# Loading the first two weight pieces behind the second attention group, and converting them behind groups 4 and 5

## The chip, the core and the metric

The kernel runs on one core of a Trainium2 chip. The metric is the device time of one execution in microseconds (us). Engines are named as in the profile: PE (matmuls), PEld (its weight loads), DVE (VectorE), ACT (ScalarE), POOL (GpSimd), SP (SyncE, which issues nearly all DMAs here). An engine's queue of issues is SPq, PEq and so on.

## The reference

An attention over (batch 4, heads 8, sequence 576, head dimension 64), half of the heads with a window of 32 keys, half with 32 keys at a distance of 4, is followed by two feed-forward layers of 512 -> 2048 -> 512 on its 2304 tokens:

```python
scores = scale * q @ k^T, masked; attn = softmax(scores); x = attn @ v
h = x @ w_in;  x = (maximum(h, 0) + alpha * minimum(h, 0)) @ w_out
h = x @ w2_in; x = (piecewise square of h) @ w2_out
```

## The kernel before

**Attention** is cut into 24 groups of three blocks. The first six groups (batch 0, `NGB` = 6, `GS` = 3) run at the start, each through the same steps: `e_scores` (PE), `e_exp` (maximum and subtract on DVE, L190 and L191, exponential on ACT, L193), `a_turn` (transposes on PE, copy on ACT, L214), `e_values` (48 small matmuls and as many weight loads on PE, L205, then `a_norm` on DVE, L229 to L231, which writes the tile `o`), `a_out` (transposes on PE, L238, copy on ACT into the big tile `XA`, L256). The score tile `s2` and the value tile `o2` have one PSUM buffer each, so the scores of a group wait until the subtract of the group before has read its tile. The loop at L804 interleaves the groups: turn i holds the scores and the exponential of group i, the transposes and the values of group i-1, the output of group i-2.

**The order is written by hand** (`manual_schedule`): every engine runs its instructions in the order of the code, and a wait at the head of an engine's queue holds up all that is behind it.

**Weights** come as 512 KB pieces of 64-bit integers. `w_load` issues a piece's DMA into a staging tile `st`, taking one of five buffers from `st_free`. `w_make` gives the three DVE steps that turn it into float32 (L321, L322, L315); `conv(k)` runs k such steps, and where a piece is finished its buffer goes back and `more()` may load the next. The last step of an input-weight piece puts it on a list; `w_cut()` then runs `w_split` for it: a copy on ACT (L327, the high half) and a subtract on POOL (L328, the low half) into a tile `wr`. `x_split` does the same for tiles of `XA`, giving `xv`. `f_h(n, f, (c,))` multiplies chunk c of weight piece f by an X tile: three PE matmuls (L513 to L515) on 128x512.

**Around the change.** Before the loop, SP is given the inputs of the six groups (`a_load_qk`, `a_load_v`, some 806 KB per group, tiles `e_in`), and behind groups 0 and 2 (`FIRST`, L58, L756) the first two weight pieces. In the loop, turns 0 and 2 end in `conv(3)` (L816), which converts one piece each. Turn 3 also splits the first X tile, clears a tile on POOL (L821) and gives SP the inputs of group 6 and all further weight pieces for which there are buffers. Turn 4 splits the second X tile. After the loop `f_h(n0, 0, (0,))` and `f_h(n0, 1, (0,))` need the two pieces; group 5's transposes, values and outputs are interleaved with the next chunks, and the main loop of slots begins, in which DVE converts the other pieces.

Of the kernel before, what the change touches and what calls it, by code (L numbers as in the profile page):

```python
# [10 lines left out]
F32 = mybir.dt.float32  # L11
# [43 lines left out]
NX = 9  # L55
NR = 4

FIRST = (0, 2)  # L58

EARLY = (5, 6)  # L60
READY = 12
# [26 lines left out]
def attention_then_two_ffns(ctx: ExitStack, tc: tile.TileContext, a0, aqk, av, w1i, w1o, w2i, w2o, alpha, masks, ident, out, out_l):  # L88
    nc = tc.nc
# [24 lines left out]
    sc_t, s_t, pT_t, o_t = {}, {}, {}, {}  # L114
# [3 lines left out]
    def a_load_qk(i):  # L118
        if i < NGB:
            nc.sync.dma_start(e_in[i][:, :QK], a0[i, :, :QK])  # L120
        elif i < NG:
            t = qk[i % 2]
            nc.sync.dma_start(t[:D, :QK], aqk[i - NGB, :D])
            nc.sync.dma_start(t[D:, KW:], aqk[i - NGB, D:])

    def a_load_v(i):
        if i < NGB:
            nc.sync.dma_start(e_in[i][:, QK:], a0[i, :, QK:])
        elif i < NG:
            for h in range(2):  # L130
                r = slice(h * D, (h + 1) * D)
                nc.sync.dma_start(vz[i % 2][r, :, h].rearrange("p n j d -> p n (j d)"), av[i - NGB, r])
# [34 lines left out]
    def e_scores(i):  # L167

        ps = ps_e.tile([P, 2, TW], F32, tag="s2", name="s_ps")
        t = e_in[i]  # L170
        mk = mask[:, i * GS:(i + 1) * GS]
        for h in range(2):
            nc.tensor.matmul(ps[:, h, :GS * KEYS].rearrange("p (n k) -> p n k", n=GS), idb, mk, start=True, stop=False)
        for n in range(GS):
            for j in range(4):
                r = slice(j * SUB, (j + 1) * SUB)
                k0 = _key_offset(i, 4 * n + j)
                for h in range(2):
                    p = slice(h * D, (h + 1) * D)
                    q = t[p, KW + n * P + j * SUB:KW + n * P + (j + 1) * SUB]  # L180
                    nc.tensor.matmul(ps[r, h, n * KEYS:(n + 1) * KEYS], q, t[p, k0:k0 + KEYS], start=False, stop=n == GS - 1)
        sc_t[i] = ps

    def e_exp(i):
        ps = sc_t.pop(i)
        s = buf(i, "s").rearrange("p (n k) -> p n k", k=KEYS)
        src = ps[:, :, :GS * KEYS].rearrange("p h (n k) -> p h n k", n=GS)
        mx = st_p.tile([P, 2 * GS], F32, tag="mx", name="mx")
        mx = mx.rearrange("p (h n) -> p h n", h=2)
        nc.vector.tensor_reduce(mx, src, AX.X, ALU.max)  # L190
        nc.vector.tensor_tensor(  # L191
            s.rearrange("p (n h) k -> p h n k", h=2), src, mx[:, :, :, None].to_broadcast([P, 2, GS, KEYS]), ALU.subtract)
        nc.scalar.activation(s, s, AF.Exp, scale=SCALE)  # L193
        s_t[i] = s

    def e_values(i):
        pT = pT_t.pop(i)
        ps = ps_e.tile([P, 2, TW], F32, tag="o2", name="o_ps")
        v = e_in[i][:, QK:].rearrange("p (n j d) -> p n j d", n=GS, j=4)
        for n in range(GS):  # L200
            for j in range(4):
                r = slice(j * SUB, (j + 1) * SUB)
                for h in range(2):
                    p = slice(h * D, (h + 1) * D)
                    nc.tensor.matmul(ps[r, h, n * DS:(n + 1) * DS], pT[p, n, r], v[p, n, j], start=True, stop=True)  # L205
        a_norm(i, ps[:, :, :GS * DS].rearrange("p h (n d) -> p n h d", n=GS))

    def a_turn(i, pool, tag):
        s = s_t.pop(i)
        ps = pool.tile([P, GS, P], F32, tag=tag, name="t_ps")  # L210
        for n in range(GS):
            nc.tensor.transpose(ps[:, n], s[:, 2 * n:2 * n + 2].rearrange("p h k -> p (h k)"), idt)  # L212
        pT = buf(i, "pT").rearrange("p (n k) -> p n k", k=P)
        nc.scalar.activation(pT, ps, AF.Copy)  # L214
        pT_t[i] = pT
# [10 lines left out]
    def a_norm(i, ps):  # L226
        o = tmp(i).tile([P, GS, 2, D], F32, tag="o", name="o")
        rs = st_p.tile([P, GS, 2, 1], F32, tag="rs", name="rs")
        nc.vector.tensor_scalar(rs, ps[:, :, :, D:], 1e-9, None, ALU.add)  # L229
        nc.vector.reciprocal(rs, rs)  # L230
        nc.vector.tensor_tensor(o, ps[:, :, :, :D], rs.to_broadcast([P, GS, 2, D]), ALU.mult)  # L231
        o_t[i] = o

    def a_out(i, pool, tag):
        o = o_t.pop(i)
        ps = pool.tile([P, GS * P], F32, tag=tag, name="x_ps")
        for n in range(GS):
            nc.tensor.transpose(ps[:, n * P:(n + 1) * P], o[:, n].rearrange("p h d -> p (h d)"), idt)  # L238
        b = i // NGB
        sb0 = (i % NGB) * GS  # L240
        subs = [x for n in range(GS) for x in _subs(sb0 + n)]
        at = 0
        while at < len(subs):
            hp, s0 = subs[at]
            n = 1
            while at + n < len(subs) and subs[at + n][0] == hp:
                n += 1
            src = ps[:, at * SUB:(at + n) * SUB]
            xb = X[hp][:, b * S:(b + 1) * S]
            p0, p1 = s0 * SUB, (s0 + n) * SUB  # L250
            if hp < NHP // 2:
                dst = xb.rearrange("p (r i) -> p i r", r=DIL)[:, p0 // DIL:p1 // DIL]
                src = src.rearrange("p (i r) -> p i r", r=DIL)
            else:
                dst = xb[:, p0:p1]
            nc.scalar.activation(dst, src, AF.Copy)  # L256
            at += n
# [7 lines left out]

    st_free = [f"v{i}" for i in range(NX - NST, NX)]

    def w_load(ph, f, part):
        w = ((w1i, w1o), (w2i, w2o))[ph][part]
        tag = st_free.pop(0)  # L270
        st = xv_p.tile([P, DM, 2], I32, tag=tag, name="st") if tag in xv_tags else pools[tag].tile([P, DM, 2], I32, tag=tag, name="st")
        nc.sync.dma_start(st.rearrange("p a b -> p (a b)"), w[f].bitcast(I32))
        cv[ph, f, part] = (st, tag)

# [83 lines left out]
    def w_split(n, f):  # L358
        t = r_slot((n, f))
        two(t[:, 0], t[:, 1], wi[n[0], f], nc.vector if n == PAIRS[0] and f < 2 else nc.gpsimd)  # L360
        wt[n, f] = t
        b = base.get((n[0], f // 2))
        if b:
            b[1] -= 1
            if not b[1]:
                x_free.append(b[0])

    def w_cut():
        while cut:
            w_split(*cut.pop(0))  # L370
# [51 lines left out]
    def x_split(n, c, on_pool=False):  # L422
        ph, t = n
        t0, w = TILES[ph][t]
        at = 0
        if w < TW and c % 2:
            x, at = xt[n, c - 1][0], w
        else:
            x = x_slot(n)
        two(x[:, 0, at:at + w], x[:, 1, at:at + w], X[c][:, t0:t0 + w], nc.gpsimd if on_pool else nc.vector)  # L430
        xt[n, c] = (x, at)
# [291 lines left out]
    def pieces(ph):  # L723

        return [(ph, 0, 0), (ph, 1, 0)] + [x for f in range(NF) for x in ((ph, f + 2, 0), (ph, f, 1)) if x[1] < NF]
# [4 lines left out]
    with tc.manual_schedule(), ExitStack() as late:  # L730
# [19 lines left out]
        pend_l = pieces(0)  # L750
        pend_w = list(pend_l)

        for i in range(NGB):
            a_load_qk(i)
            a_load_v(i)
            if i in FIRST:  # L756
                w_load(*pend_l.pop(0))
            if i == 1:
                nc.sync.dma_start(mask[:, 2 * GS:], masks[:, 2 * GS:])
        nc.sync.dma_start(al, alpha)  # L760
# [11 lines left out]
        def fill(n):  # L772

            for _ in range(n):
                nc.tensor.matmul(warm_ps, warm[:, :P], warm, start=True, stop=True)
# [11 lines left out]
        def conv(k):  # L787

            for _ in range(k):
                if not todo and pend_w and pend_w[0] in cv:  # L790
                    todo.extend(w_make(*pend_w.pop(0)))
                if todo:
                    todo.pop(0)()
                    if not todo:
                        more()
# [8 lines left out]
        for i in range(NGB):  # L804
            e_scores(i)
            if i >= 1:
                a_turn(i - 1, ps_a, "a")
            e_exp(i)
            if i >= 2:
                a_out(i - 2, ps_a, "w")  # L810
            else:
                fill(2)
            if i >= 1:
                e_values(i - 1)
            w_cut()
            if i in FIRST:  # L816
                conv(3)
            if i == 3:
                x_split(n0, 0, True)

                nc.gpsimd.memset(qk[0], 0.0)  # L821
                hold = False
                a_load_qk(NGB)
                w_load(*pend_l.pop(0))
                w_load(*pend_l.pop(0))
                a_load_v(NGB)
                more()
            if i == 4:
                x_split(n0, 1, True)
# [394 lines left out]
```

## Time and profile before

| | us |
|---|---|
| median of 3 runs | 848.47 (847.82 to 849.39) |
| profiled execution, its own time | 848.41 |
| span of its instructions | 846.3 |
| PE busy | 831.4 (98%) |
| DVE busy | 514.4 (61%) |
| ACT busy | 459.3 (54%) |
| POOL busy | 483.1 (57%) |
| mean granted TensorE clock | 0.996 |

The span runs from the first to the last instruction; 2.1 us of the execution's own time lie outside. A share of busy time is a mean over stages with different limits: the start, with small attention tiles and the first weights, is the only part in which PE is not busy throughout. Times of rows are us from the start of the span. A chain piece called "issue" is time in which the engine waited for nothing that the profile shows. The releaser in brackets is inferred. Matmul ends are modelled.

### The profile page before, as it was taken

The numbers are of one execution on the slowest core, as the hardware profiler recorded it, in microseconds if no ns is written. First come the engines' busy times: TensorE is split into PE (matmuls) and PEld (weight loads), VectorE is DVE, ScalarE is ACT, GpSimd is POOL, SyncE is SP. The second block draws the span as 40 slices with busy tenths as digits, with TensorE's granted clock in tenths as the row PEclk, the third lists the DMA queues.
The fourth block names the chain that finished last, engine by engine and source line by source line (L and its number), as shares of the span: only waits on it lengthen the run. The fifth ranks groups of instructions, "written<-read, shape, count | busy, mean of one in ns | idle before, by whom it ended". The sixth has DMA issues, their size and how long they took to land.

```text
span 846.3 us, 14045 instructions
## 1 busy us (share of the span) xinstructions
PE 831.4 (98%) x5232; PEld 681.3 (81%) x5234; DVE 514.4 (61%) x831; ACT 459.3 (54%) x883; POOL 483.1 (57%) x411
## 2 busy tenths in 40 slices
PE   6999999999999999999999999999999999999998
PEld 3667778998777878888888888888888888888897
DVE  4798787666775676776688565665326556530132
ACT  3444444665435465555444677675437666553375
POOL 2465656777434677767448676754662332346485
PEclk9899999999999999999999999999999999999999
DMA  8788665864640025444287735343835553538120
GB/s 303 240 252 228 203 171 179 257 196 135 191 129 26 1 75 180 144 154 169 100 312 301 282 142 204 127 173 121 327 125 203 196 198 125 174 134 313 69 82 25
DMA packets 54978, 147.43 MB, mean 174 GB/s; under 512 B 5632, under 2 KB 13440, under 8 KB 54912
## 3 DMA queue, kind: packets, MB, share of 16 engines
q1 hardware_dynamic: 54624, 146.39, 50.9%
q8 instruction: 41, 0.67, 0.3%
q14 instruction: 25, 0.20, 0.1%
q10 hardware_dynamic: 288, 0.16, 0.1%
HBM read 101.97 MB, written 44.56 MB: 173 GB/s over the span
## 4 chain that ended last, share of the span: by engine, by line
PE 92%; DVE 4%; ACT 1%; issue 1%; DMA 1%; ACTq 0%; DVEq 0%
PE y L706 14%; PE y L707 14%; PE y L708 14%; PE h_ps L544 9%; PE h_ps L546 9%; PE h_ps L545 9%; PE h_ps L513 5%; PE h_ps L515 5%; PE h_ps L514 5%; PE o_ps L223 2%; PE s_ps L149 1%; PE t_ps L212 1%; PE y L691 1%; PE y L692 1%; PE y L693 1%
## 5 line engine op out<-in xcount | busy, mean ns | idle before, releaser
L328 POOL TENSOR_TENSOR wol<-wo,woh 128x512 fp32r<-128x512 f32 x153 | 201.8, 1326 | 74.5 <-ACT woh L327 64.4
L328 POOL TENSOR_TENSOR wr<-wb,wr 128x512 fp32r<-128x512 f32 x60 | 77.8, 1297 | 130.3 <-ACT wr L327 130.3
L706 PE MATMUL y<-gh,wol 128*128 128x512 f32 (+1 forms) x384 | 146.3, 381 | 0.0
L708 PE MATMUL y<-gl,woh 128*128 128x512 f32 (+1 forms) x384 | 142.8, 372 | 0.0
L707 PE MATMUL y<-gh,woh 128*128 128x512 f32 (+1 forms) x384 | 142.8, 372 | 0.0
L328 POOL TENSOR_TENSOR wr<-wi,wr 128x512 fp32r<-128x512 f32 x50 | 64.6, 1293 | 121.2 <-ACT wr L327 119.9
L544 PE MATMUL h_ps<-xv,wr 128*128 128x512 f32 x336 | 131.3, 391 | 0.5 <-DVE gl L666 0.4
L546 PE MATMUL h_ps<-xv,wr 128*128 128x512 f32 x336 | 130.8, 389 | 0.0
L545 PE MATMUL h_ps<-xv,wr 128*128 128x512 f32 x336 | 130.8, 389 | 0.0
L327 ACT ACTIVATE woh<-wo 128x512 fp32r<-128x512 f32 x153 | 93.5, 626 | 65.7 <-PE y L708 51.3
L513 PE MATMUL h_ps<-xv,wr 128*128 128x512 f32 (+1 forms) x256 | 89.9, 351 | 0.2
L514 PE MATMUL h_ps<-xv,wr 128*128 128x512 f32 (+1 forms) x256 | 86.3, 337 | 0.2 <-DVE xv L328 0.2
L515 PE MATMUL h_ps<-xv,wr 128*128 128x512 f32 (+1 forms) x256 | 86.4, 337 | 0.0
L706 PEld LDWEIGHTS y<-gh,wol 128*128 128x128 f32 x384 | 72.2, 188 | 15.2 <-issue 2.0
L708 PEld LDWEIGHTS y<-gl,woh 128*128 128x128 f32 x384 | 72.2, 188 | 13.0 <-DVE gl L581 0.4
L707 PEld LDWEIGHTS y<-gh,woh 128*128 128x128 f32 x384 | 72.3, 188 | 11.8
L544 PEld LDWEIGHTS h_ps<-xv,wr 128*128 128x128 f32 x336 | 63.1, 188 | 15.8 <-issue 1.4
L706 PE MATMUL y<-gx,wol 128*128 128x512 f32 x192 | 74.8, 390 | 0.0
L707 PE MATMUL y<-gx,woh 128*128 128x512 f32 x192 | 74.7, 389 | 0.0
L708 PE MATMUL y<-gx,woh 128*128 128x512 f32 x192 | 74.7, 389 | 0.0
L566 DVE SCALAR_TENSOR_TENSOR h_ps<-h_ps,g 128x512 f32<-128x512 f32 x64 | 44.6, 697 | 48.3 <-ACT g L558 48.3
L546 PEld LDWEIGHTS h_ps<-xv,wr 128*128 128x128 f32 x336 | 63.1, 188 | 13.2
(130 smaller groups left out, 1552.3 us busy)
## 6 DMA issues: line engine op xcount, KB each, us to landing
gd<-XA SPq DMA_DIRECT2D x42, 512.0 KB, 3.3
gx<-gd SPq DMA_DIRECT2D x42, 512.0 KB, 6.5
wb<-whole SPq DMA_DIRECT2D x30, 512.0 KB, 5.1
st<-w1i SPq DMA_DIRECT2D x16, 512.0 KB, 5.2
st<-w1o SPq DMA_DIRECT2D x16, 512.0 KB, 5.3
st<-w2i SPq DMA_DIRECT2D x16, 512.0 KB, 4.2
st<-w2o SPq DMA_DIRECT2D x16, 512.0 KB, 4.9
kept<-wr SPq DMA_DIRECT2D x16, 512.0 KB, 2.7
```

Source lines behind the costliest of these rows:

```text
L327: nc.scalar.activation(hi, src, AF.Copy)
L328: low_on.tensor_tensor(lo, src, hi.bitcast(F32), ALU.subtract)
L513: nc.tensor.matmul(ps[:, :w], r[:, 1, cs], x[:, 0, xs], start=(c == 0), stop=False)
L514: nc.tensor.matmul(ps[:, :w], r[:, 0, cs], x[:, 1, xs], start=False, stop=False)
L515: nc.tensor.matmul(ps[:, :w], r[:, 0, cs], x[:, 0, xs], start=False, stop=(c == NC - 1))
L544: nc.tensor.matmul(o, w[:, 1, cs], x[:, 0], start=start and m == 0, stop=False, skip_group_check=not start)
L545: nc.tensor.matmul(o, w[:, 0, cs], x[:, 1], start=False, stop=False, skip_group_check=not start)
L546: nc.tensor.matmul(o, w[:, 0, cs], x[:, 0], start=False, stop=m == 1, skip_group_check=not start)
L566: ve.scalar_tensor_tensor(ps, ps, 1.0, t, ALU.max, ALU.min)
L706: nc.tensor.matmul(o, wl[:, cs], gh[:, :w], start=(i == 0), stop=False)
L707: nc.tensor.matmul(o, wh[:, cs], gh[:, :w], start=False, stop=False)
L708: nc.tensor.matmul(o, wh[:, cs], gl[:, :w], start=False, stop=(i == NF - 1))
```

## The change

The first two weight pieces are no longer loaded with the inputs of groups 0 and 2. Turn 2 of the loop loads both, behind the normalisation of group 1 (the second group): ahead of each DMA, DVE copies one element per partition of that group's output `o_t[1]` into the piece's staging tile, and the DMA, which overwrites it, has to wait for that copy. `FIRST` now names turns 3 and 4, so one piece is converted at the end of turn 3 and one at the end of turn 4; each is split by the `w_cut` of the turn behind.

```diff
-FIRST = (0, 2)
+FIRST = (3, 4)
...
-    def w_load(ph, f, part):
+    def w_load(ph, f, part, behind=None):
         w = ((w1i, w1o), (w2i, w2o))[ph][part]
         tag = st_free.pop(0)
...
+        if behind is not None:
+            nc.vector.tensor_copy(st[:, 0, :1].bitcast(F32), behind[:, 0, 0, :1])
         nc.sync.dma_start(st.rearrange("p a b -> p (a b)"), w[f].bitcast(I32))
...
         for i in range(NGB):
             a_load_qk(i)
             a_load_v(i)
-            if i in FIRST:
-                w_load(*pend_l.pop(0))
...
             if i >= 1:
                 e_values(i - 1)
+            if i == 2:
+                for _ in FIRST:
+                    w_load(*pend_l.pop(0), o_t[1])
             w_cut()
             if i in FIRST:
                 conv(3)
```

## Rows read from the trace of the kernel before

**Rows 1.** Busy time by stage: us, busy (instructions) per engine, PEclk, DMA share, GB/s

```profile
35.40:57.30 21.90, 19.76 (x151) 14.32 (x151) 21.16 (x36) 9.96 (x19) 12.85 (x10) 1.00 0.97 284
57.30:846.35 789.05, 784.43 (x4426) 649.18 (x4426) 474.57 (x754) 434.43 (x835) 459.96 (x387) 1.00 0.49 167
```

**Rows 2.** Chain that ended last, first 80 us: start us, us, what

```profile
17.66 3.08 issue
...
34.76 0.69 DVE xv L328
...
54.35 0.66 DVE g L653
```

**Rows 3.** Timeline of PE: start us, us, engine line, operation, tiles, [idle before, releaser]

```profile
14.47 0.72 PE L205 MATMUL o_ps<-e_in,pT 64*32 64x65 f32 x48 [1.63 <-ACT s L193]
...
17.23 0.42 PE L205 MATMUL o_ps<-e_in,pT 64*32 64x65 f32 x23 [0.32 <-ACT pT L214]
...
20.74 0.66 PE L205 MATMUL o_ps<-e_in,pT 64*32 64x65 f32 x25 [3.08 <-issue]
...
29.11 0.39 PE L513 MATMUL h_ps<-xv,wr 128*128 128x512 f32 x1
```

**Rows 4.** Busy time between the two stalls: us, then PE, PEld, DVE, ACT, POOL

```profile
14.46:18.00 3.54, 2.88 (x127) 2.13 (x126) 2.64 (x7) 0.58 (x2) 0.00 (x0) 1.00 1.03 401
```

**Rows 5.** DMA queues, 18.20 to 18.29 us: packets, MB, share of 16 engines

```profile
q8 instruction: 1, 0.02, 76.7%
```

**Rows 6.** DMA queues, 21.70 to 21.80 us

```profile
q8 instruction: 1, 0.02, 55.3%
```

**Rows 7.** Half-microsecond slices: us, PE busy (instructions), PEclk, DMA share, GB/s

```profile
17.50:18.00 0.50, 0.16 (x19) 1.00 1.03 383
18.00:18.50 0.50, 0.00 (x0) 1.00 0.63 171
...
19.50:20.00 0.50, 0.00 (x0) 0.88 0.09 20
...
26.50:27.00 0.50, 0.50 (x4) 0.79 1.02 320
```

**Rows 8.** Timeline of DVE around groups 1 to 4

```profile
15.22 0.17 DVE L229 TENSOR_SCALAR rs<-o_ps 128x6 f32<-128x6 f32 x1 [1.93 <-PE o_ps L205]
...
15.65 0.56 DVE L231 TENSOR_TENSOR o<-o_ps,rs 128x384 f32<-128x384 f32 x1
...
16.12 0.42 DVE L321 TENSOR_SCALAR wi<-st 128x512 int32<-128x512 int32 x1
...
17.91 0.55 DVE L190 TENSOR_REDUCE mx<-s_ps 128x6 f32<-128x384 f32 x1
...
22.77 0.56 DVE L190 TENSOR_REDUCE mx<-s_ps 128x6 f32<-128x384 f32 x1 [0.32 <-PE s_ps L181]
...
23.43 0.56 DVE L191 TENSOR_TENSOR s<-s_ps,mx 128x384 f32<-128x384 f32 x1
```

**Rows 9.** DMA issues, stretches 57 to 59, 55 to 57, 25.7 to 25.8: KB, us to landing

```profile
st<-w1o SPq DMA_DIRECT2D x1, 512.0 KB, 3.5
...
st<-w1i SPq DMA_DIRECT2D x1, 512.0 KB, 3.9
...
st<-w1i SPq DMA_DIRECT2D x1, 512.0 KB, 4.7
```

**Rows 10.** Timeline of POOL and DVE at 35 us

```profile
35.32 1.28 POOL L328 TENSOR_TENSOR wr<-wi,wr 128x512 fp32r<-128x512 f32 x1 [8.05 <-ACT wr L327]
35.37 1.52 DVE L321 TENSOR_SCALAR wo<-st 128x512 int32<-128x512 int32 x1
```

**Rows 11.** Timeline of ACT and POOL: the split of the second piece, group 5's exponential

```profile
20.18 0.62 ACT L327 ACTIVATE wr<-wi 128x512 fp32r<-128x512 f32 x1
...
20.88 1.27 POOL L328 TENSOR_TENSOR wr<-wi,wr 128x512 fp32r<-128x512 f32 x1 [7.42 <-ACT wr L327]
...
27.74 0.52 ACT L193 ACTIVATE s<-s 128x384 f32<-128x384 f32 x1 [0.15 <-DVE s L191]
...
28.17 0.47 ACT L256 ACTIVATE XA<-x_ps 128x384 f32<-128x384 f32 x1
```

**Rows 12.** DMA queues, 12.10 to 12.19 us

```profile
q8 instruction: 1, 0.02, 76.9%
```

## The prediction

> **What bounds the kernel now.** I read the stages first, then the chain that ended last, then the timelines of the single engines, and last the DMA queues and the clock in short slices. [rows 1] shows two stages. From 57.3 us to the end PE is busy 784.4 of 789.1 us: a shift of this stage's start is a shift of the end, and little can absorb it. From 35.4 to 57.3 DVE is busy 21.16 of 21.90 us, and the chain of [rows 2] goes through it from `xv` at 34.76 to `g` at 54.35. So the question is when DVE reaches the `xv` step at 34.76 (the low half of the fourth X tile), and everything before that counts only as far as it moves this point.
>
> What leads up to it is a chain over the six groups. In it PE loses time twice between two instructions of one run of equal matmuls, in `e_values`: up to 14.47, and from 17.66 to 20.74, 3.08 us [rows 3]. The second is no data wait: 23 of the 48 matmuls had read the same tiles before it. Between the ends of the two stalls PE and its weight loads ran 127 + 126 = 253 instructions [rows 4], and a packet of the instruction queue, started at 18.2 us, took 0.767 x 0.09 us x 16 engines = 1.10 us [rows 5], so PE went on 1.4 us after it. A packet of 16 KB started at 21.7 to 21.8, with the data queue empty [rows 6], and stopped nobody. I read both stalls as instruction fetch behind the group inputs. The clock fell in the second: granted 1.00 until about 19.9, 0.50 until about 26.7, that is 1.2 instead of 2.4 GHz [rows 7].
>
> **The change part by part.** *Two loads leave the front of SP's queue*: 2 x 512 KB. In [rows 7] the bulk of the inputs ends at about 18.2, and the 0.5 us slices before it run near 400 GB/s, so what is behind both loads comes 1.05 MB / 400 GB/s = 2.6 us sooner. For groups 0 to 2 this buys nothing: their scores already wait for PE or DVE, and values of group 1 still meet the first stall, ending 14.47. The next fetch, asked for about then, finds the queue draining from 15.6 on. Its packet took from 14.47 to 18.2 to start before; unloaded, 20.74 to 21.7, 1.0 us. The end of the second stall so lies between 14.47 + 1.0 + 1.1 + 1.4 = 18.0 and 20.7; I take 18.3, nearest to the unloaded row since the backlog is gone. PE gains 2.4 us there, and the clock does not fall at 19.9.
>
> *Two conversions leave DVE in groups 0 and 2*, each three steps, 16.12 to 17.91 = 1.8 us [rows 8]. The first hid behind PE. Without the second the maximum of group 3 moves from 17.91 to 16.5. Their `w_split` steps on ACT and POOL go too; POOL had room.
>
> *Two one-element copies* on DVE, behind group 1's `o`, which ends at 15.65 + 0.56 = 16.21 [rows 8]. Nearest row: 128x6 in 0.17 us [rows 8]; from nothing to 0.17 each, I take 0.12, so SP issues the first load at 16.45 (before: 1.66). Queued behind it on SP are the second load and the group-6 inputs, which wait for a POOL memset anyway. DVE goes on with group 3's maximum, whose scores are done: 0.24 us, hidden.
>
> *The loads land.* A 512 KB load into a quiet queue took 3.5 and 3.9 us, a third one 4.7 [rows 9]. I take 3.9: the first piece is there at 20.35 (19.95 to 21.15), the second 1.3 us of transfer later.
>
> *Two conversions enter DVE in front of the maximum of group 4 and of group 5*, and this is the wait that the change adds: DVE stands at the first step for the DMA, and behind it are queued group 4's maximum and subtract, group 3's normalisation, the second conversion, and group 5's steps; PE's next scores wait for the subtract, since they share one PSUM tile. Group 2's `o` ends at about 18.3 + 0.4 for the rest of the matmuls + 1.0 = 19.7, so DVE stands still until 20.4. The first conversion takes 1.85 us from there. Its first step may meet POOL, which then splits the first X tile. [rows 10] show such a meeting: the step took 1.52 us beside a POOL operation of 1.28 us, against 0.42 us alone [rows 8]; cost 0 to 1.1, I take 0.45, since the POOL step has begun earlier by then. The rest by the steps of before:
>
> First conversion ends 20.4 + 1.85 + 0.45 = 22.7. Group 4's maximum and subtract, 22.77 to 23.99 before [rows 8], 1.22: 23.9. Normalisation of group 3, 15.22 to 16.21, 0.99: 24.9. Second conversion, landed, 1.85: 26.8. Group 5's maximum and subtract, 1.22: 28.0. On ACT the exponential and the copy of group 3's output, 27.74 to 28.64, 0.90: 28.9 [rows 11]. Then `w_split` of the second piece, ACT then POOL, 20.18 to 22.15, 1.97 [rows 11]: 30.9.
>
> There `f_h(n0, 1, (0,))` starts, which needs that piece; before it began at 29.11 [rows 3]. PE, which passes groups 4 and 5 in order, has nothing to put in its place: the transpose of group 5, its values, the next `f_h` chunks and the outputs are queued behind, and they lead to the `xv` step at 34.76. So the gain on PE (2.4 us and the clock) ends in front of a weight that is 1.8 us later than the old chain. Bounds: landing at 19.95 and no meeting with POOL give +0.9; landing at 21.15 with a full meeting +3.3.
>
> DVE's order after that is unchanged, its loads (third piece on) are issued earlier, since the memset on POOL comes sooner, so all of the 1.8 us go through the DVE stage and PE's stage. Sum: 848.41 + 1.8 = 850.2 for the profiled execution, and the median is 0.06 higher: **850.3 us**, +0.2%.
>
> **The rivals.** (a) *The clock falls in the new wait.* PE has done group 4's values and `f_h(n0, 0, (0,))` by about 28.2 and then waits some 2.7 us for the second piece, and a little earlier another 2 us for the subtract of group 4. The row for it: 2.2 us into the 3.08 us stall the clock went to 1.2 GHz and stayed there 6.8 us [rows 7]. For it: nearly the same idle time. Against it: before the old fall PE had also been idle or in 32-wide tiles, here a full-width `f_h` stands ahead of the wait. If it falls, the PE work from `f_h(n0, 1, (0,))` to group 5's output, some 3.5 us, runs at up to half speed: 25 of the values' matmuls took 0.66 us slow, 23 took 0.42 us fast [rows 3]. That is 0 to 3.0 us more, 2.2 likely: 848.4 + 1.8 + 2.2 + 0.1 = 852.5.
>
> (b) *The stall stays.* That PE's stall is a fetch behind data is my reading of [rows 3 to 6]. The Trainium skill ("Runtime: NRT & Kernel Launch", Instruction fetch mechanics) says that the sequencer fetches the next 16 KiB block while it runs the present one and that crossing a block is mostly hidden. By that rule the 3.08 us would have another cause, and the change need not remove it. In rows: values of group 2 then end at 21.4 as before, DVE starts the first conversion at 22.5, ends it at 24.35, and the second piece is split 8.2 us later, at 32.5: +3.4, 851.9. The trace speaks against the rule with 3.08 us at a distance of 253 instructions, but the depth of the backlog that a fetch meets is not seen.
>
> (c) *Not slower: the first stall shrinks too.* Its packet started at 12.1 us [rows 12], in the bulk of the inputs; with the first weight load gone, the fetch may be served sooner. The price is at most the idle time before 14.47 less what PE would have waited anyway, 1.4 us, and it moves the copies, the loads and all that hangs on them: 850.3 - 1.4 = 848.9. It decides once more than 1.0 us of that stall goes. Against it: the queue stays full until 15.6 with group inputs instead.
>
> (d) *Faster.* If the second piece were split before PE has done `f_h(n0, 0, (0,))`, at about 27.5, PE would pass without a wait and 1.5 to 2 us and the rest of the slow clock would be won: about 846.3. That needs the first piece landed by 17.1; issued at 16.45 it would have to land in 0.7 us, where the rows give 3.5. Only a shorter first stall together with a chain that is less tight than my steps could do it.
>
> **How the numbers follow.** 0.2% is 1.7 us, about what a measurement of this kernel can tell from no change. Forecast 0.36 (849.4 to 852.1, with its middle just past the bound: 0.16 within, 0.20 slower), clock 0.30, stall stays 0.10, first stall shrinks 0.14, faster 0.10. Slower 0.60, within 0.30, faster 0.10. The range leaves out the faster case and the top of the clock case: 847.8 to 853.4.
>
> **What would show it.** In the profile after: the stall in `e_values` of group 2 shorter by 2 us or more and the clock at 1.00 through 20 to 25; DVE waiting for a DMA at the first conversion, landing near 20.4, group 4's maximum near 22.7; PE waiting for POOL's `wr` ahead of the second `f_h`, at about 30.9; the `xv` step near 36.5 and everything after it shifted by the same. I am wrong if that `f_h` does not wait for `wr`, if the stall moves to another place, or if the clock falls between 28 and 32.

## The result, and the profile after

| | before | after |
|---|---|---|
| median, us | 848.5 | 853.62 (852.79 to 853.99) |
| ratio after / before | | 1.0056 (1.0043 to 1.0069) |
| profiled execution, its own time | 848.41 | 853.8 |
| span | 846.3 | 852.0 |

The change costs 0.56%, some 5 us. Nearly all of it arises in the first 40 us. The fourth X tile, on which the argument turned, is split by DVE at 40.00 instead of 34.76 [rows 2], 5.24 us later; the transposes with which PE's stage begins come at 62.56 instead of 57.31, 5.25 us later (the two lines below, before and after, are of the chains that ended last); and behind that the stages are the same work as in [rows 1].

```profile
57.31 0.55 PE t_ps L212 x3
...
62.56 0.55 PE t_ps L212 x3
```

Stages of the changed kernel (us, then busy time and instructions of PE, PEld, DVE, ACT, POOL):

```profile
40.69:62.56 21.87, 19.74 (x152) 14.33 (x152) 21.13 (x35) 9.98 (x19) 12.78 (x10) 1.00 0.88 259
62.56:852.05 789.49, 784.45 (x4426) 649.11 (x4426) 474.70 (x754) 435.14 (x835) 459.95 (x387) 1.00 0.49 167
```

The chain that ended last, in order of time (start us, us, what). Lines below L273 are two or three higher than before: L323, L324, L317 are the three conversion steps, L329 and L330 the two of a split, L515 the first matmul of `f_h`:

```profile
16.55 3.63 DMA st<-w1i
20.20 2.03 DVE wi L323
...
23.67 0.48 DVE mx L190
...
28.43 0.48 DVE mx L190
...
30.50 0.53 ACT wr L329
...
31.09 1.27 POOL wr L330
...
40.00 0.69 DVE xv L330
```

The chain of before ran over PE's stall here; now it runs from the load through both conversions, group 4's and group 5's maxima and the split of the second piece into the second `f_h`, as the changed order says. The engines' timelines show the same with what each waited for:

```profile
16.36 0.21 DVE L273 COPY st<-o 128x1 f32<-128x1 f32 x2
...
18.39 0.43 PE L205 MATMUL o_ps<-e_in,pT 64*32 64x65 f32 x25 [0.61 <-issue]
...
19.56 1.27 POOL L330 TENSOR_TENSOR xv<-XA,xv 128x512 fp32r<-128x512 f32 x1 [14.72 <-ACT xv L329]
...
20.20 2.02 DVE L323 TENSOR_SCALAR wi<-st 128x512 int32<-128x512 int32 x1 [0.29 <-DMA st<-w1i]
...
20.77 1.17 POOL L824 MEMSET qk<- 128x1280 f32 x1
...
23.06 0.30 PE L205 MATMUL o_ps<-e_in,pT 64*32 64x65 f32 x3 [1.55 <-issue]
...
24.86 0.50 PE L173 MATMUL s_ps<-mask,idt 128*128 128x192 bf16 x2 [1.50 <-DVE s L191]
...
26.60 1.28 POOL L330 TENSOR_TENSOR wr<-wi,wr 128x512 fp32r<-128x512 f32 x1 [4.66 <-ACT wr L329]
26.79 1.65 DVE L317 SCALAR_TENSOR_TENSOR wi<-st,wi 128x512 int32<-128x512 int32 x1
...
27.84 1.72 POOL L330 TENSOR_TENSOR xv<-XA,xv 128x512 fp32r<-128x512 f32 x1
...
32.41 0.80 PE L515 MATMUL h_ps<-xv,wr 128*128 128x512 f32 x1 [2.19 <-POOL wr L330]
...
33.85 0.84 PE L212 MATMUL t_ps<-idt,s 128*128 128x128 f32 x3
```

The stall of 3.08 us in the values of group 2 [rows 3] has shrunk to 0.61, ending at 18.39. A new one of 1.55 us stands in the values of group 3, and behind it PE waits 1.50 us for DVE's subtract of group 4. DVE waits 0.29 us for the first piece. Its first step then takes 2.02 us beside POOL, the last step of the second piece 1.65 us beside POOL, and the second `f_h` waits for POOL's split and starts at 32.41 (before: 29.11). In half-microsecond slices (us, PE busy, granted clock, DMA share, GB/s) the clock no longer falls at 19.9 but at about 23.9, and comes back only at 37.5:

```profile
23.50:24.00 0.50, 0.00 (x0) 0.88 0.76 266
...
32.50:33.00 0.50, 0.50 (x1) 0.50 1.00 401
...
37.50:38.00 0.50, 0.50 (x3) 0.97 0.00 0
```

So of 5.24 us, 32.41 - 29.11 = 3.3 are there when the second `f_h` starts, and 5.24 - 3.30 = 1.94 come between it and the X tile, where PE runs at 1.2 GHz until 37.5, which ran at 2.4 before.

### The profile page after: what moved, and what is told of

It reads as the page before. It is cut to its first block, busy times and chain, and to the rows that moved or that the text cites. A ratio compares the mean times of both kernels' runs of the same rounds, so it can differ in the third digit from the quotient of the medians.

```text
span 852.0 us, 14053 instructions
## 1 busy us (share of the span) xinstructions
PE 834.4 (98%) x5234; PEld 682.9 (80%) x5234; DVE 517.0 (61%) x833; ACT 460.1 (54%) x883; POOL 483.6 (57%) x411
## 4 chain that ended last, share of the span: by engine, by line
PE 88%; DVE 6%; ACT 2%; POOL 1%; issue 1%; DMA 1%; SPq 0%; DVEq 0%; ACTq 0%; POOLq 0%
PE y L708 14%; PE y L709 14%; PE y L710 13%; PE h_ps L546 8%; PE h_ps L547 8%; PE h_ps L548 8%; PE h_ps L515 5%; PE h_ps L517 5%; PE h_ps L516 5%; PE o_ps L223 2%; PE s_ps L149 1%; PE y L693 1%; PE y L694 1%; PE y L695 1%; PE t_ps L212 1%
## 5 line engine op out<-in xcount | busy, mean ns | idle before, releaser
L330 POOL TENSOR_TENSOR wol<-wo,woh 128x512 fp32r<-128x512 f32 x153 | 201.8, 1326 | 74.5 <-ACT woh L329 64.3
L330 POOL TENSOR_TENSOR wr<-wb,wr 128x512 fp32r<-128x512 f32 x60 | 77.7, 1295 | 130.5 <-ACT wr L329 130.5
L329 ACT ACTIVATE woh<-wo 128x512 fp32r<-128x512 f32 x153 | 93.8, 628 | 65.7 <-PE y L710 51.3
L330 POOL TENSOR_TENSOR wr<-wi,wr 128x512 fp32r<-128x512 f32 x50 | 64.6, 1293 | 112.9 <-ACT wr L329 111.6
L515 PE MATMUL h_ps<-xv,wr 128*128 128x512 f32 (+1 forms) x256 | 90.9, 355 | 2.4 <-POOL wr L330 2.2
```

The lines of the kernel that those rows point to most:

```text
L329: nc.scalar.activation(hi, src, AF.Copy)
L330: low_on.tensor_tensor(lo, src, hi.bitcast(F32), ALU.subtract)
L515: nc.tensor.matmul(ps[:, :w], r[:, 1, cs], x[:, 0, xs], start=(c == 0), stop=False)
```

## The experiments

The theory at this point: the conversions stand in the chain of the last groups (3.3 us, part of it a wait of DVE for POOL), and the slow clock behind it costs 1.9. The rivals: the late arrival of the loads; a clock that costs nothing beside a DVE-bound stage; a chain that DVE holds and PE's wait only hides. Ratios are against the kernel before on the same chip, with their 95% interval. The runs were made on several chips, and the medians of the kernel before on them lie between 847.6 and 848.5 us; so where two versions are compared, the ratios say how much was gained (0.1% is 0.85 us).

**Conversions late, loads early.** The loads go back to where they were, without the copies; only the place of the conversions differs from the kernel before.

```diff
+            if i in (0, 2):
+                w_load(*pend_l.pop(0))
...
-            if i == 2:
-                for _ in FIRST:
-                    w_load(*pend_l.pop(0), o_t[1])
```

> The two loads stand in SP's queue as before the change (behind the inputs of groups 0 and 2, no copies), only the two conversions stay at the end of turns 3 and 4. Theory (the conversions stand in the chain of the last groups, the loads' landing adds little): the stall in the values of group 2 is back to about 20.7 us, the first conversion starts near 22.5 without waiting for a DMA, the second f_h starts at 33 to 35 us (before the change 29.1, after it 32.4), and the whole takes 853 to 856 us. Rival (the loss is the wait for the late loads): both pieces have landed by 15 us, so nothing of the loss is left, 848 to 849.5 us.

Measured: 853.88 us, 1.0065 (1.0048 to 1.0083). Timelines of DVE and PE:

```profile
20.90 0.43 PE L205 MATMUL o_ps<-e_in,pT 64*32 64x65 f32 x25 [2.19 <-issue]
...
22.33 0.42 DVE L323 TENSOR_SCALAR wi<-st 128x512 int32<-128x512 int32 x1
...
27.31 1.64 DVE L317 SCALAR_TENSOR_TENSOR wi<-st,wi 128x512 int32<-128x512 int32 x1
...
32.93 0.80 PE L515 MATMUL h_ps<-xv,wr 128*128 128x512 f32 x1 [2.89 <-POOL wr L330]
```

The stall ends at 20.90, nearly as before the change, no step waits for a DMA, and yet the second `f_h` starts at 32.93 and the time is that of the whole change. The place of the conversions alone makes the loss, and the rival is out. In sum the late loads neither win nor lose: with them the stall ends 2.5 us sooner (18.39) and the first conversion starts 2.1 us sooner (20.20), but its first step then meets POOL and takes 2.02 us, where here, behind POOL's two operations, it takes 0.42. So only 0.5 us of the lead is left at the second `f_h`, and nothing of it at the end.

**Matmuls in PE's waits.** Five on a constant tile behind the values of group 3, eight ahead of the first `f_h`.

```diff
+            if i == 4:
+                fill(5)
             w_cut()
...
         w_cut()
+        fill(8)
         f_h(n0, 0, (0,))
```

> The changed kernel with matmuls on a constant tile, whose results nobody reads, where PE stands idle: 5 behind the values of group 3 and 8 ahead of the first f_h. Theory (of the 5.2 us that the change costs at the last X tile, 3.3 are the second f_h's wait for its weight and 1.9 are the slow clock behind that): the granted clock stays at 1.00 or comes back before the second f_h at about 32.4, which itself does not move, and the whole is 1 to 2 us faster than the changed kernel, 851.5 to 852.6. Rival (the clock costs nothing, since DVE sets the pace there): the same as the changed kernel, 853.2 to 854, with the clock at 1.00 or not.

Measured: 851.87 us, 1.0035 (1.0022 to 1.0048). PE's slices (us, PE busy, granted clock, DMA share, GB/s) and its second `f_h`:

```profile
24.00:25.00 1.00, 1.00 (x4) 0.53 0.98 316
...
27.00:28.00 1.00, 0.86 (x6) 0.76 0.89 303
```

```profile
32.65 0.50 PE L515 MATMUL h_ps<-xv,wr 128*128 128x512 f32 x1 [1.35 <-POOL wr L330]
...
38.39 0.69 DVE L330 TENSOR_TENSOR xv<-XA,xv 128x512 fp32r<-128x512 f32 x1 [0.19 <-ACT xv L329]
```

The clock still falls, but is back at about 27.5. The second `f_h` starts nearly where it did, the X tile comes at 38.39 instead of 40.00, and the whole is 853.6 - 851.9 = 1.7 us faster (by the ratios 0.21%, 1.8 us). From the second `f_h` to the X tile it is now 38.39 - 32.65 = 5.74 us at the full clock, against 7.59 in the changed kernel and 5.65 before. That is the clock's price, and the rival, by which it costs nothing, is out.

**The conversions' intermediate result in PSUM** (where the matmuls' results lie; the weights' tiles lie in SBUF). Each step then has one SBUF input at most.

```diff
             if i in FIRST:
+                w0_tile[0] = lambda: ps_h.tile([P, DM], F32, tag="h", name="w_ps")
                 conv(3)
+                w0_tile[0] = None
```

> The changed kernel with the intermediate result of the two conversions in PSUM instead of SBUF (the tile of h, which is free then), so that each conversion step has at most one SBUF input. In the changed kernel the first step of the first conversion took 2.02 us beside two POOL operations (0.42 alone), and the last step of the second took 1.65 us (0.69 alone). Theory (they wait for POOL over the SBUF port that both use): the first step takes 0.69, the last 0.70, the second f_h comes 1.9 to 2.4 us sooner, at 30.0 to 30.5, and the whole takes 850.5 to 852. Rival (the step was long for another reason, such as its own DMA still landing): the steps stay long and the time stays within 0.5 us of 853.6.

Measured: 851.8 us, 1.0037 (1.0024 to 1.005). DVE, POOL and PE:

```profile
20.12 0.69 DVE L323 TENSOR_SCALAR w_ps<-st 128x512 int32<-128x512 int32 x1
...
20.91 1.17 POOL L826 MEMSET qk<- 128x1280 f32 x1
...
25.18 1.28 POOL L330 TENSOR_TENSOR wr<-wi,wr 128x512 fp32r<-128x512 f32 x1 [3.10 <-ACT wr L329]
...
25.65 0.69 DVE L317 SCALAR_TENSOR_TENSOR wi<-st,w_ps 128x512 int32<-128x512 int32 x1
...
26.42 1.28 POOL L330 TENSOR_TENSOR xv<-XA,xv 128x512 fp32r<-128x512 f32 x1
...
30.32 0.80 PE L515 MATMUL h_ps<-xv,wr 128*128 128x512 f32 x1 [2.65 <-POOL wr L330]
...
38.08 0.69 DVE L330 TENSOR_TENSOR xv<-XA,xv 128x512 fp32r<-128x512 f32 x1 [0.96 <-ACT xv L329]
```

POOL runs the same operations beside both steps, and the steps are short: 2.02 and 1.65 become 0.69. The second `f_h` starts 2.1 us sooner, and 1.8 us of that reach the end (by the ratios 0.19%, 1.6 us). The Trainium skill ("SBUF — State Buffer", SBUF: two separate sides) says that DVE and POOL share one pair of ports, which an operation holds from start to end, and that a DVE operation needs it in its two-port mode or with two SBUF inputs while POOL reads SBUF. These rows agree: 2.02 and 1.65 us beside POOL, 0.69 for both with PSUM in between. The wait of 2.65 us for the split remains, and the clock falls in it, at about 29.0.

**Half of the change.** The first piece as before the change; only the second late, converted at the end of turn 3.

```diff
-FIRST = (3, 4)
+FIRST = (0, 3)
...
+            if i == 0:
+                w_load(*pend_l.pop(0))
...
             if i == 2:
-                for _ in FIRST:
-                    w_load(*pend_l.pop(0), o_t[1])
+                w_load(*pend_l.pop(0), o_t[1])
```

> Half of the change: the first piece is loaded and converted as before the change (behind group 0), only the second piece is loaded behind group 1's output and converted at the end of turn 3. Theory (the loss comes from the second conversion of the changed kernel, which stands in front of group 5's maximum and is split last): one conversion at turn 3 delays group 4's maximum to 23 to 24 us, nothing stands in front of group 5's, and the second f_h does not wait for its weight and starts at 27.5 to 29 us: 846 to 848.5 us. Rival (any load behind group 1's output arrives too late): the second f_h waits for its weight at 30 us or later, 850 us or more.

Measured: 848.62 us, 1.0009 (0.9998 to 1.002). The matmuls of both first `f_h` on PE:

```profile
29.54 0.63 PE L517 MATMUL h_ps<-xv,wr 128*128 128x512 f32 x1
29.97 0.63 PE L515 MATMUL h_ps<-xv,wr 128*128 128x512 f32 x1
```

The second follows the first without a wait. A piece that is loaded behind group 1's output and converted at turn 3 is in time; the loss hangs on the second late conversion, at turn 4. A start at 29.97 is later than the 27.5 to 29 that were expected. In this profile the clock was at 1.2 GHz from about 20.5 to 30.8, having fallen 0.9 us after the end of a stall that still lasts 1.70 us; it is the profile of the slowest execution, 852.21 us, and not typical. The median is just above the expected range, 846 to 848.5.

**Group inputs late instead of weights.** In the kernel before, the inputs of group 5 (806 KB) are taken from the front of SP's queue and loaded behind group 1's output.

```diff
-            a_load_qk(i)
-            a_load_v(i)
+            if i < NGB - 1:
+                a_load_qk(i)
+                a_load_v(i)
...
+            if i == 2:
+                for c in (0, QK):
+                    nc.vector.tensor_copy(e_in[NGB - 1][:, c:c + 1], o_t[1][:, 0, 0, :1])
+                a_load_qk(NGB - 1)
+                a_load_v(NGB - 1)
```

> The kernel before, its weights untouched; instead the inputs of group 5 (806 KB, first needed near 23 us) are taken out of the front of SP's queue and loaded behind group 1's output with two one-element copies. Theory (what the change wins on PE, the shorter stall in the values of group 2 and the clock, is real, and is lost only because the late piece is a weight on the chain): the stall ends at 18.5 to 19.3 instead of 20.7, the clock stays at 1.00 or nearly, the second f_h starts at 25.5 to 27.5 instead of 29.1, and the whole takes 844.5 to 847. Rival (the relief of the stall is worth nothing, since another wait takes its place before the last X tile): 848 to 849 us.

Measured: 849.1 us (846.42 to 850.88), 1.0011 (1.0001 to 1.0021). Its profile is of the fastest execution, 846.42:

```profile
19.21 0.66 PE L205 MATMUL o_ps<-e_in,pT 64*32 64x65 f32 x25 [1.00 <-issue]
...
33.53 0.69 DVE L328 TENSOR_TENSOR xv<-XA,xv 128x512 fp32r<-128x512 f32 x1
```

There the stall is 1.00 us and the X tile 1.2 us sooner than before, as the theory has it, though the clock did not stay at 1.00 (it was at 0.50 from about 15.6 to 22.4). The median, however, is not below that of before, and above the 848 to 849 of the rival. The theory of a gain misses, and why stays open: of the slower executions only the span and the mean granted clock are known, and the clock (0.993 to 0.999) does not follow their times.

**PSUM and matmuls in the waits together.**

> The changed kernel with both edits that helped it: the conversions' intermediate result in PSUM, and the 13 matmuls on a constant tile in PE's waits. Theory (three costs that add: the wait over the shared SBUF port 1.8 us, the clock 1.8, the rest of the wait for the second piece 1.2 to 1.6): the second f_h at 30 to 30.5 and the clock at 1.00 there, 849.6 to 850.6 us. Rival (the two edits win the same time): 851.5 to 852 us, as each alone.

Measured: 849.06 us, 1.0014 (1.0006 to 1.0023).

```profile
30.18 0.50 PE L515 MATMUL h_ps<-xv,wr 128*128 128x512 f32 x1 [0.76 <-POOL wr L330]
...
35.91 0.69 DVE L330 TENSOR_TENSOR xv<-XA,xv 128x512 fp32r<-128x512 f32 x1 [0.19 <-ACT xv L329]
```

Of the 0.56% that the change costs, 0.42 are back, some 3.6 us; alone the two edits gave 0.21 and 0.19. So they do not win the same time: within the noise, they add. The median lies half a us below the range expected, 849.6 to 850.6.

**The second `f_h` behind group 5's values.**

```diff
         f_h(n0, 0, (0,))
-        f_h(n0, 1, (0,))
         a_turn(NGB - 1, ps_a, "a")
...
+        f_h(n0, 1, (0,))
         f_h(n0, 0, (1,))
```

> The changed kernel with the second f_h (n0, 1, (0,)) moved from ahead of group 5's transposes to behind its values; nothing else. Theory (what holds the chain is PE's in-order wait for the second piece's split, with group 5 queued behind it): group 5's transposes start near 30.2 instead of 33.9, the last X tile is split by DVE at 37.5 to 38.7 instead of 40.0, since the slow clock stays, and the whole takes 851 to 852.5 us. Rival (the chain is held by DVE's conversions and group 5's subtract, which PE's wait only hides): the last X tile stays within 0.5 us of 40.0 and the time within 0.5 us of 853.6.

Measured: 850.17 us, 1.0029 (1.0018 to 1.0041).

```profile
29.90 0.90 PE L212 MATMUL t_ps<-idt,s 128*128 128x128 f32 x3 [0.15 <-ACT s L193]
...
32.29 0.77 PE L515 MATMUL h_ps<-xv,wr 128*128 128x512 f32 x1
...
36.44 0.69 DVE L330 TENSOR_TENSOR xv<-XA,xv 128x512 fp32r<-128x512 f32 x1 [1.13 <-ACT xv L329]
```

DVE's conversions are as in the changed kernel, and the `f_h` itself starts at the same time (32.29), but group 5's transposes no longer stand behind it: 29.90 instead of 33.85. The X tile is 3.6 us sooner, and sooner than expected, since PE, being busy, had the full clock back by 33 (37.5 in the changed kernel). The whole is about 0.27% faster by the ratios, 2.3 us; the medians, which are of two chips, differ by 3.4, more than the 1.1 to 2.6 that the expected times amount to. So it is PE's in-order wait that holds the chain, not DVE; a wait of 0.15 us for group 5's exponential is all that is left of DVE's part there.

**All edits, and the first step of the next piece to be converted behind the loop in PSUM too.** The expectations call it the third piece; by the tiles in the rows (`wo`, L321 in [rows 10]) it is the fourth.

> All edits that should help at once: the changed kernel with the conversions' intermediate result in PSUM (that of the third weight piece behind the loop too, whose first step took 1.52 us beside POOL before and after), the 13 matmuls on a constant tile, and the second f_h behind group 5's values. Theory (the costs are these, and without them the late loads leave at most the shorter stall): the last X tile at 34 to 35.2 us and the pieces behind it 0.8 us sooner, 847 to 848.3 us, at or just below the kernel before. Rival (the late loads cost more than these edits can give back): 849 us or more, as with the first two edits alone.

Measured: 847.9 us, 1.0000 (0.9991 to 1.0009).

```profile
35.13 0.69 DVE L330 TENSOR_TENSOR xv<-XA,xv 128x512 fp32r<-128x512 f32 x1 [0.89 <-ACT xv L329]
...
35.74 0.69 DVE L323 TENSOR_SCALAR w_ps<-st 128x512 int32<-128x512 int32 x1
```

With all edits the changed kernel is the kernel before to within a tenth of a per cent. They take back the whole loss, and nothing of the shorter stall is left as a gain. How the loss divides among them is less sure: alone the first three gave 0.21, 0.19 and 0.27%, 0.67 in sum against the 0.56 of the loss, which within their intervals may be an overlap or nothing; and whether matmuls in the waits or the new order would also help the kernel before was not tried.

**That last edit alone, on the kernel before.**

```diff
         w_cut()
+        w0_tile[0] = lambda: ps_a.tile([P, DM], F32, tag="w", name="w_ps")
         conv(1)
```

> The kernel before with one edit: the third weight piece's intermediate result goes to PSUM already (this step took 1.52 us beside POOL, before the change and after it), everything else as before. Theory (DVE sets the pace from the last X tile on, so what is saved in its queue there is saved in the whole): the step takes 0.69, the pieces behind it come 0.8 us sooner, and the time is 0.5 to 0.9 us below the kernel before. Rival (the stage behind it absorbs what DVE gains): within 0.3 us of the kernel before.

Measured: 848.23 us, 1.0003 (0.9994 to 1.0012).

```profile
35.26 0.69 DVE L321 TENSOR_SCALAR w_ps<-st 128x512 int32<-128x512 int32 x1
...
35.86 0.68 DVE L848 TENSOR_SCALAR al<-al 128x16 f32<-128x16 f32 x1
...
36.80 0.75 DVE L653 SCALAR_TENSOR_TENSOR g<-g,al,h_ps 128x512 f32<-128x512 f32 x1 [0.27 <-ACT g L650]
```

The step is short, but the 0.8 us are not won: the small step behind it, which is also SBUF to SBUF, meets POOL in its place (0.68 us for 16 elements), and `g` waits for ACT anyway. The theory misses here: a busy DVE is not a chain in which every step counts. (The profile is of the slowest execution, 849.7 us.)

**Half of the change with PSUM.**

> The half change (only the second piece late, converted at the end of turn 3) with that conversion's and the third piece's intermediate result in PSUM. Theory (with one conversion in front of group 4 only, and no wait over the SBUF port, half of the change costs nothing and keeps part of the shorter stall): second f_h behind the first one without a wait for its weight, 846.3 to 847.7 us, below the kernel before by 0.3 to 1.5 us. Rival (a late piece costs as much as the shorter stall gives, whatever else is done): the kernel before less the 0.8 us of the third piece at most, 847 to 848.5 us, with no gain over the run with that one edit alone.

Measured: 847.8 us, 0.9995 (0.9986 to 1.0004): no gain that can be told from the kernel before, and the median is above the 846.3 to 847.7 of the theory. In the profile the second `f_h` does follow the first without a wait (28.04, 28.28), and the X tile comes at 33.91. No version beat the kernel before.

## Why the prediction was right or wrong

The forecast was 850.3 us and slower by 0.2%; measured were 853.62, slower by 0.56%. By the ratio, 848.47 x 1.0056 = 853.2, it lies at the top of the range given, 847.8 to 853.4; the median itself is 0.2 above it. That it comes so near the range is owed to the room left for rival (a), the clock, which came true on top of a first term that was sized too small. At the X tile, 5.24 us are the 1.8 of the forecast, 1.5 more of the first term and 1.94 of the clock.

- **Bound and chain: right.** The X tile's shift, 5.24 us, is found again at PE's stage (5.25).
- **Fetch stall: right where it was, but a second one came.** Forecast to end at 18.3, it ended at 18.39. A packet of the instruction queue started at 15.8 to 15.9 instead of 18.2 [rows 5], once the inputs had drained, and PE went on about 1.4 us after its end, as before. With the loads early again (the first experiment) the stall ended at 20.90. So rival (b), that it stays, is out: with less data in the queue it shrank from 3.08 to 0.61 us. That the stalls are fetches is still inferred from these packets. The trace does not agree with the Trainium skill ("Runtime: NRT & Kernel Launch", Instruction fetch mechanics), by which crossing a block is mostly hidden. DMA queues of the changed kernel, 15.80 to 15.90 and 20.70 to 20.80 us:

```profile
q8 instruction: 1, 0.02, 71.8%
...
q8 instruction: 1, 0.02, 56.1%
```

- **Another stall, not forecast**: 1.55 us up to 23.06, inside the values of group 3, 253 recorded instructions of PE and its weight loads after the end of the first, the distance of [rows 4] again. Its packet, the second in the rows above, started at 20.7, behind the two loads. A stall that moves to another place was one of the prediction's own signs of being wrong. DVE was later still, so it costs nothing on the chain; but it lengthened the idle time in which the clock fell.
- **Copies and landing: right.** Both copies 0.21 us, the load issued at 16.55, landed 3.6 us later, DVE's wait 0.29.
- **Wait for POOL: the step that failed.** I put 0.45 us on one meeting, since POOL would have begun its split before. POOL had indeed begun, 0.64 us earlier, but the step met the split and the memset queued behind it, which the sum leaves out: 2.02 - 0.42 = 1.6. The second conversion met POOL too, which I had not looked for, since I had placed its first step and not its last: 1.65 - 0.69 = 0.96. The two are 2.1 us above my term; the rest of the chain went about 0.6 faster than by my steps, so the second `f_h` was late by 3.3 instead of 1.8. That the upper bound that I gave, 3.3, was met exactly is luck: it held a late landing and one meeting, and what came were a landing on time and two meetings, one of them with two operations. With the meetings taken away the second `f_h` comes at 30.32, where my sum without them gives 30.9 - 0.45 = 30.45.
- **Clock: the right mechanism, in the rival, and at another place.** 2.2 us were put on it, 1.94 measured between the second `f_h` and the X tile, and 1.7 by the run with matmuls in the waits. I held it for less likely than not, and expected it between 28 and 32. It fell at 23.9, 0.5 us into the earlier of the two waits that rival (a) names, that for group 4's subtract. PE had been idle for 2.1 of the 2.4 us before, 1.55 of them in the stall that I had not forecast, so the reasoning covers the fall only in part. The wait for the second piece came while the clock was low, and the full clock came back only 5.1 us after it. That this wait can bring the fall is seen in two other runs, in which the clock was at 1.00 ahead of it: with the loads early it fell in the wait of 2.89 us, and with PSUM alone in that of 2.65 us:

```profile
32.00:32.50 0.50, 0.00 (x0) 0.90 1.02 410
...
29.00:29.50 0.50, 0.00 (x0) 0.50 1.04 298
```

- **Chances.** Rivals (c) and (d) had nothing for them: the first stall ended at 14.59 (14.47 before), and PE waited 2.19 us ahead of the second `f_h`.

## What to carry to other kernels

A step moved out of an early stage lands in front of something; write down what is queued behind its new place on its own engine and on the engines that wait for it, to the end of the chain, with every engine that shares a port with it in that stretch. A stall that is shortened pays only if the next thing in order is ready, so find what is late next before counting the gain. Where an in-order engine must wait for a late operand, putting independent work ahead of the wait (2.3 us here, by the ratios) can be worth more than making the operand earlier (1.6 us).

## What was not expected of the hardware

- A DVE step can wait out two POOL operations in a row: 2.02 us from 20.20, beside POOL operations of 1.27 us from 19.56 and 1.17 us from 20.77. DVE did not come in between: the step ended 0.28 us after the second of them. The reordered kernel shows the same (2.19 us).
- A DVE step with two SBUF inputs also lengthened (1.65 for 0.69 us), and POOL's next operation beside it as well (1.72 for 1.28 us); with one of the inputs in PSUM both were short (0.69 and 1.28).
- The same instructions differ in where the clock falls, from one profile to another. The run with the last edit alone has the same program as the kernel before up to 35 us, yet its clock fell at 16.5 and not at 19.9. The reordered kernel has that of the changed one up to the second `f_h`, yet its clock fell at 15.8 and again at 26.1, and not at 23.9. The times of one version on one chip spread by 0.8 to 4.5 us, with this or with something else that single profiles do not show.
